# Token-major norm, an integer float64-to-float32 conversion, 1 KB loads and a fixed engine order in a linear-attention and gated feed-forward kernel

## The chip, the cores and the metric

The kernel runs on one core of one Trainium2 chip. The metric is the device time of one execution in microseconds (us), as the median of several executions. A profile shows one such execution; its span is some 2 us shorter than the device time.

TensorE (PE in the profile) multiplies matrices, PEld is its weight load, VectorE (DVE) and ScalarE (ACT) do elementwise work, GpSimd (POOL) likewise, and SyncE (SP) issues the transfers (DMA).

## The reference

```python
# q, k, v: 8 batches x 8 heads x 576 tokens x 64, float32; w1, w2: 512 x 1024, w3: 1024 x 1024,
# w_out: 1024 x 512. The four weights arrive as float64.
kv  = einsum('bhsd,bhse->bhde', k, v)
o   = einsum('bhsd,bhde->bhse', q, kv)
o   = o / sqrt(mean(o*o, axis=-1) + 1e-6) * g_norm          # norm of each token and head
x   = o.transpose(0, 2, 1, 3).reshape(8 * 576, 512)
out = ((x @ w1) * (x @ w2)) @ w3 @ w_out                     # 4608 x 512
```

Both kernels compute `w3 @ w_out` once ("the fold") and then need, for each group of 512 tokens, the gates (`x w1` times `x w2`, eight blocks of 128 features) and one projection. There are nine groups: the first 512 tokens of each batch, and one that gathers the 64 tokens left over in each.

## The kernel before

The conversion takes float64 as raw 32-bit words. Six of its operations are VectorE's, one is ScalarE's, two are GpSimd's.

```python
def convert(dst, src):                       # 128 partitions x 512 values, 40 times
    raw = fold.tile([P, c, n], I64, name="raw", bufs=3)
    nc.sync.dma_start(out=raw, in_=src)
    ...
    nc.scalar.activation(rest, lo, AF.Copy, scale=2.0 ** -52)
    nc.vector.tensor_scalar(out=bits, in0=hi, scalar1=0x7FFFFFFF, ..., op0=ALU.bitwise_and)
    nc.vector.tensor_scalar(out=power, in0=power, scalar1=LEAST, scalar2=MOST, ...)   # clamp
    ...                                      # three more on VectorE
    nc.vector.tensor_scalar(out=bits, in0=dst_bits, scalar1=0xFF800000, ...)
    nc.gpsimd.tensor_tensor(out=rest, in0=rest, in1=power, op=ALU.mult)
    nc.gpsimd.tensor_tensor(out=dst, in0=dst, in1=rest, op=ALU.add)

w1_sb = const.tile([P, NP, DF], FP32, name="w1_sb")       # NP = 4 strips of DF = 1024 columns
def convert_gates(f):
    cols = slice(f * P, (f + 1) * P)                      # block f: 128 columns of each strip
    for dst, src in ((w1_sb, w1), (w2_sb, w2)):
        convert(dst[:, :, cols], src[:, cols].rearrange("(c p) f -> p c f", p=P))
```

The norm works on features in partitions. A matmul with a matrix of 1/64 gives every feature the mean of its head, and the root and reciprocal run on 128x512:

```python
nc.tensor.matmul(ms_ps[:, 0:n], lhsT=mean_bd, rhs=sq[:, 0:n], start=True, stop=True)
nc.scalar.activation(inv[:, 0:n], ms_ps[:, 0:n], AF.Sqrt, bias=eps_col)
nc.vector.reciprocal(inv[:, 0:n], inv[:, 0:n])
nc.vector.scalar_tensor_tensor(out=dst, in0=src, scalar=g_col, in1=by, op0=ALU.mult, op1=ALU.mult)
```

The order in the program is not the order on the engines here: a scheduler in the compiler moves instructions within each engine's queue as the dependencies allow.

```python
for T in range(NG):                    # the gates of group T, with pieces of attention T+1 between
    for f in range(KF):
        gate(T, f)
        if T == 0: convert_out(f)
        if f < len(pieces): pieces[f]()
    ...
    if T == 0:
        turn_w3(0)                     # convert and transpose one block of w3
        for i in range(KF):
            if i + 1 < KF: turn_w3(i + 1)
            fold_block(i)
    project(T)
```

Of the kernel before, what the change touches and what calls it, by code (L numbers as in the profile page):

```python
# [14 lines left out]
ALU = mybir.AluOpType  # L15


@with_exitstack
def kernel(
# [12 lines left out]
    """Linear attention with per-head RMS norm, then ((x w1) * (x w2)) (w3 w_out), all in fp32.  # L32

    Weights of float64 come as their raw words and are rounded to fp32 on the chip.
    Activations stay transposed (features on partitions) from the attention to the gates.
    A group of tokens is the first 512 of one batch; the last group gathers the 64 tokens
    left over in each batch.
    """
# [7 lines left out]
    NP = H // 2          # pairs of heads: 128 features each  # L46
    KF = DF // P
    J = 4
    G = J * P            # tokens of a group
    L = S - G            # tokens left over in a batch  # L50
    KR = 96              # rows of k and v on partitions
    KJ = S // KR
    NG = B + 1
    assert D == 64 and DM == NP * P and DM == 512 and B * L == G and S % KR == 0
# [12 lines left out]
    def load_batch(b):  # L67
        k_sb = inp.tile([KR, H, KJ, D], FP32, name="k_sb")
        v_sb = inp.tile([KR, H, KJ, D], FP32, name="v_sb")
        for dst, src in ((k_sb, k), (v_sb, v)):  # L70
            nc.sync.dma_start(
                out=dst.rearrange("p h j d -> p h (j d)"),
                in_=src[b].rearrange("h (p j) d -> p h (j d)", j=KJ),
            )
        q_sb = inp.tile([P, J, H, D], FP32, name="q_sb")
        for j in range(J):
            nc.sync.dma_start(  # L77
                out=q_sb[:, j], in_=q[b, :, j * P:(j + 1) * P, :].rearrange("h p d -> p h d")
            )
        ql_sb = inp.tile([L, H, D], FP32, name="ql_sb")  # L80
        nc.sync.dma_start(out=ql_sb, in_=q[b, :, G:S, :].rearrange("h p d -> p h d"))
        return q_sb, ql_sb, k_sb, v_sb

    loaded = {0: load_batch(0)}

    g_col = const.tile([P, 1], FP32, name="g_col")
    g_src = g_norm.rearrange("(d o) -> d o", o=1)
    for e in range(2):
        nc.sync.dma_start(out=g_col[e * D:(e + 1) * D, :], in_=g_src)
# [7 lines left out]
    # |hi| is clamped to the exponents that fp32 has, so far smaller values become 0. Its low  # L97
    # 27 bits and the top bit of its exponent then make the fp32 with a 20-bit mantissa, and
    # lo, scaled by the power of two in it, is added with one rounding.
# [4 lines left out]
    def convert(dst, src):  # L104
        if src.dtype == FP32:
            nc.sync.dma_start(out=dst, in_=src)
            return
        c, n = dst.shape[1:]
        raw = fold.tile([P, c, n], I64, name="raw", bufs=3)
        nc.sync.dma_start(out=raw, in_=src)  # L110
        words = raw.bitcast(U32).rearrange("p c (n w) -> p c n w", w=2)
        lo, hi = words[:, :, :, 0], words[:, :, :, 1]
        power = fold.tile([P, c, n], FP32, name="power")
        rest = fold.tile([P, c, n], FP32, name="rest")
        bits, dst_bits = power.bitcast(U32), dst.bitcast(U32)
        nc.scalar.activation(rest, lo, AF.Copy, scale=2.0 ** -52)  # L116
        nc.vector.tensor_scalar(  # L117
            out=bits, in0=hi, scalar1=0x7FFFFFFF, scalar2=None, op0=ALU.bitwise_and
        )
        nc.vector.tensor_scalar(  # L120
            out=power, in0=power, scalar1=LEAST, scalar2=MOST, op0=ALU.max, op1=ALU.min
        )
        nc.vector.tensor_scalar(  # L123
            out=bits, in0=bits, scalar1=3, scalar2=0x40000000,
            op0=ALU.logical_shift_left, op1=ALU.bitwise_xor,
        )
        nc.vector.tensor_scalar(  # L127
            out=dst_bits, in0=hi, scalar1=0x80000000, scalar2=None, op0=ALU.bitwise_and
        )
        nc.vector.scalar_tensor_tensor(  # L130
            out=dst_bits, in0=bits, scalar=0x7FFFFFFF, in1=dst_bits,
            op0=ALU.bitwise_and, op1=ALU.bitwise_or,
        )
        nc.vector.tensor_scalar(  # L134
            out=bits, in0=dst_bits, scalar1=0xFF800000, scalar2=None, op0=ALU.bitwise_and
        )
        nc.gpsimd.tensor_tensor(out=rest, in0=rest, in1=power, op=ALU.mult)  # L137
        nc.gpsimd.tensor_tensor(out=dst, in0=dst, in1=rest, op=ALU.add)  # L138

    def convert_gates(f):  # L140
        cols = slice(f * P, (f + 1) * P)
        for dst, src in ((w1_sb, w1), (w2_sb, w2)):
            convert(dst[:, :, cols], src[:, cols].rearrange("(c p) f -> p c f", p=P))

    def convert_out(f):
        convert(wo_sb[:, f:f + 1, :], w_out[f * P:(f + 1) * P, :].rearrange("p (c f) -> p c f", c=1))

# [5 lines left out]
    mean_bd = const.tile([P, P], FP32, name="mean_bd")  # L153
    nc.vector.memset(mean_bd, 0.0)
    for e in range(2):
        rows = slice(e * D, (e + 1) * D)
        nc.vector.memset(mean_bd[rows, rows], 1.0 / D)
    kv_bd = [const.tile([P, NP, P], FP32, name=f"kv_bd{i}") for i in range(2)]
    for t in kv_bd:
        nc.vector.memset(t, 0.0)  # L160

# [4 lines left out]
    def attention(b):  # L166
        q_sb, ql_sb, k_sb, v_sb = loaded.pop(b)
        bd = kv_bd[b % 2]
        qT = work.tile([P, NP, S], FP32, name="qT", bufs=1)
        x = xT[b] = work.tile([P, NP, G], FP32, name="xT")  # L170

        def kv():
            kv_ps = bank(ps_at, "at")[:, 0:NP * D].rearrange("p (r e) -> p r e", r=NP)
            for r in range(NP):
                for j in range(KJ):
                    for e in range(2):
                        nc.tensor.matmul(  # L177
                            kv_ps[e * D:(e + 1) * D, r, :],
                            lhsT=k_sb[:, 2 * r + e, j, :],
                            rhs=v_sb[:, 2 * r + e, j, :],  # L180
                            start=(j == 0),
                            stop=(j == KJ - 1),
                        )
            for e in range(2):
                rows = slice(e * D, (e + 1) * D)
                nc.vector.tensor_copy(out=bd[rows, :, rows], in_=kv_ps[rows])

        def q_t(r):
            qt_ps = bank(ps_at, "at")
            for j in range(J):  # L190
                nc.tensor.transpose(  # L191
                    qt_ps[:, j * P:(j + 1) * P], q_sb[:, j, 2 * r:2 * r + 2, :], ident
                )
            nc.scalar.copy(qT[:, r, 0:G], qt_ps)

        def q_t_left():
            qt_ps = bank(ps_at, "at")[:, 0:NP * L].rearrange("p (r t) -> p r t", r=NP)
            for r in range(NP):
                nc.tensor.transpose(
                    qt_ps[:, r, :], ql_sb[:, 2 * r:2 * r + 2, :], ident[0:L, 0:L]  # L200
                )
            nc.scalar.copy(qT[:, :, G:S], qt_ps)
# [3 lines left out]
        def product(r):  # L206
            """o = q kv of one pair of heads (of all, for the tokens left over), and its squares"""
            o_ps = bank(ps_at, "at")
            n = G
            if r < NP:  # L210
                nc.tensor.matmul(o_ps, lhsT=bd[:, r, :], rhs=qT[:, r, 0:G], start=True, stop=True)  # L211
            else:
                n = NP * L
                for i in range(NP):
                    nc.tensor.matmul(
                        o_ps[:, i * L:(i + 1) * L],
                        lhsT=bd[:, i, :],
                        rhs=qT[:, i, G:S],
                        start=True,
                        stop=True,  # L220
                    )
            sq = work.tile([P, G], FP32, name="sq")
            nc.scalar.activation(sq[:, 0:n], o_ps[:, 0:n], AF.Square)  # L223
            st[r] = o_ps, sq, n

        def norm(r):
            """x = o * g / sqrt(mean(o^2) + eps); the means reach every feature of their head"""
            o_ps, sq, n = st.pop(r)
            ms_ps = bank(ps_at, "at")
            nc.tensor.matmul(ms_ps[:, 0:n], lhsT=mean_bd, rhs=sq[:, 0:n], start=True, stop=True)  # L230
            inv = sq
            nc.scalar.activation(inv[:, 0:n], ms_ps[:, 0:n], AF.Sqrt, bias=eps_col)  # L232
# [166 lines left out]
```

## Time and profile before

| | before |
|---|---|
| device time, median of three | 1032.11 us (1030.88 to 1033.82) |
| span of the profiled execution | 1029.5 us |
| PE busy | 937.1 us (91%) |
| VectorE / ScalarE / GpSimd busy | 377.0 / 153.0 / 108.0 us |
| first gate matmul / first fold block / end of the fold | 52.7 / 185.7 / 260.8 us |

The stages are read from two views: PE in order of time, and the chain of waits (the chain that ended last, from start to end). The busy share of the whole span hides that two stages have different limits. The groups of the page show who holds whom in the front. Each row has the line, engine, operation, output and inputs, shapes and count; then the busy us and the mean ns of one; then the idle time just ahead, with its releaser:

```profile
L137 POOL TENSOR_TENSOR rest<-rest,power 128x512 f32<-128x512 f32 x40 | 53.1, 1334 | 135.5 <-DVE power L134 130.3
L138 POOL TENSOR_TENSOR w_sb<-w_sb,rest 128x512 f32<-128x512 f32 x32 | 43.5, 1366 | 1.6
L268 PE MATMUL mm<-xT,w_sb 128*128 128x512 f32 x1024 | 457.0, 600 | 38.6 <-DVE xT L240 38.6
```

GpSimd waits 130.3 us in all for the last VectorE operation of a unit (one piece of 128x512 values), so the conversion is a chain over both engines. The gate matmuls (L268), however, are not seen to wait for weights. Their 38.6 us are spent waiting for `xT`, the last operation of the norm, which stands in the same VectorE queue as the conversion and the wide reciprocals. So it is VectorE's queue as a whole that sets when gates can run; what the conversion's share is worth is measured below (55 us).

### The profile page before, as it was taken

The page shows a single profiled execution, that of the slowest core. Times are in us where ns is not written, and L with a number is a line of the kernel's source. Part 1 is how long each engine was busy: PE and PEld are TensorE (multiplying, and loading weights), DVE is VectorE, ACT ScalarE, POOL GpSimd, SP SyncE. Part 2 cuts the span into 40 slices and gives each one's busy share as a digit, 9 for nine tenths or more (in the row PEclk, how much of TensorE's full clock was granted, in tenths as well). Part 3 has the DMA queues.
Part 4 walks back from the last instruction along what each step waited for, and adds up shares of the span by engine and source line. Part 5 has one row for each costly group of instructions (what it writes and reads, how often), then busy time and mean ns, then how long its engine had stood idle before and what let it go on. Part 6 is the DMA issues. An engine that isn't in the chain of part 4 may idle for free.

```text
span 1029.5 us, 7522 instructions
## 1 busy us (share of the span) xinstructions
PE 937.1 (91%) x3056; PEld 438.9 (43%) x3056; DVE 377.0 (37%) x448; ACT 153.0 (15%) x260; POOL 108.0 (10%) x86
## 2 busy tenths in 40 slices
PE   3138869788999999999999999999999999999997
PEld 3014425333444445444444544454444444444443
DVE  2999897884003501440053025113501440000100
ACT  2222223210001101110120122012101210000000
POOL 0555550543000000000000000000000000000000
PEclk9668969899999999999999999999999999999999
DMA  9854741830000016002500420051010000001001
GB/s 199 214 143 140 182 128 33 212 116 3 20 21 0 0 41 133 6 8 61 111 0 21 108 51 0 29 115 35 1 41 1 0 21 20 1 0 41 0 1 41
DMA packets 67075, 59.21 MB, mean 58 GB/s; under 512 B 38880, under 2 KB 59360, under 8 KB 67040
## 3 DMA queue, kind: packets, MB, share of 16 engines
q1 hardware_dynamic: 67040, 58.73, 22.7%
q8 instruction: 24, 0.39, 0.2%
q14 instruction: 11, 0.09, 0.0%
HBM read 49.28 MB, written 9.44 MB: 57 GB/s over the span
## 4 chain that ended last, share of the span: by engine, by line
PE 81%; DVE 11%; issue 3%; POOL 2%; SPq 2%; DMA 1%; ACT 0%; POOLq 0%; DVEq 0%
PE mm L268 45%; PE mm L318 24%; PE mm L306 4%; PE at L230 2%; PE at L211 2%; DVE power L117 2%; DVE power L123 1%; PE at L177 1%; DVE power L120 1%; DVE w_sb L130 1%; DVE w_sb L127 1%; POOL w_sb L138 1%; SPq L77 1%; DVE sq L233 1%; PE at L191 1%
## 5 line engine op out<-in xcount | busy, mean ns | idle before, releaser
L268 PE MATMUL mm<-xT,w_sb 128*128 128x512 f32 x1024 | 457.0, 600 | 38.6 <-DVE xT L240 38.6
L268 PEld LDWEIGHTS mm<-xT,w_sb 128*128 128x128 f32 x1024 | 195.6, 193 | 280.6 <-issue 258.7
L318 PE MATMUL mm<-w3o_sb,ab 128*128 128x512 f32 x576 | 250.0, 593 | 0.0
L279 DVE TENSOR_TENSOR ab<-a_sb,mm 128x512 f32<-128x512 f32 x72 | 49.5, 687 | 414.1 <-PE mm L268 382.7
L318 PEld LDWEIGHTS mm<-w3o_sb,ab 128*128 128x128 f32 x576 | 109.0, 190 | 132.3 <-issue 130.3
L233 DVE RECIPROCAL sq<-sq 128x512 f32<-128x512 f32 (+1 forms) x40 | 120.2, 3020 | 21.4 <-ACT sq L232 21.4
L277 ACT COPY a_sb<-mm 128x512 f32<-128x512 f32 x72 | 42.1, 585 | 279.7 <-PE mm L268 279.7
L137 POOL TENSOR_TENSOR rest<-rest,power 128x512 f32<-128x512 f32 x40 | 53.1, 1334 | 135.5 <-DVE power L134 130.3
L328 DVE COPY o_sb<-mm 128x512 f32<-128x512 f32 x18 | 12.5, 692 | 145.0 <-PE mm L318 145.0
L306 PE MATMUL mm<-wo_sb,w3T 128*128 128x512 f32 x128 | 58.0, 609 | 0.0
L268 PE MATMUL mm<-x_left,w_sb 128*128 128x512 f32 x128 | 55.1, 592 | 0.0
L230 PE MATMUL at<-sq,mean_bd 128*128 128x512 f32 (+1 forms) x80 | 41.6, 604 | 11.1 <-ACT sq L223 11.1
L326 ACT COPY o_sb<-mm 128x512 f32<-128x512 f32 x18 | 10.5, 586 | 252.7 <-PE mm L318 252.7
L116 ACT ACTIVATE rest<-raw 128x512 f32<-128x512 uint32 x40 | 27.2, 680 | 129.1 <-POOL w_sb L138 100.0
L138 POOL TENSOR_TENSOR w_sb<-w_sb,rest 128x512 f32<-128x512 f32 x32 | 43.5, 1366 | 1.6
L232 ACT ACTIVATE sq<-at,eps_col 128x512 f32<-128x512 f32 (+1 forms) x40 | 25.7, 644 | 105.8 <-PE at L230 105.6
L177 PE MATMUL at<-v_sb,k_sb 96*64 96x64 f32 x768 | 26.3, 234 | 15.1 <-DMA v_sb<-in_v_dram 14.1
L211 PE MATMUL at<-qT,kv_bd 128*128 128x512 f32 x64 | 35.6, 639 | 2.5 <-DVE xT L240 1.8
L268 PEld LDWEIGHTS mm<-x_left,w_sb 128*128 128x128 f32 x128 | 24.3, 190 | 30.6 <-issue 30.6
L306 PEld LDWEIGHTS mm<-wo_sb,w3T 128*128 128x128 f32 x128 | 24.6, 197 | 28.4 <-issue 28.4
L117 DVE TENSOR_SCALAR power<-raw 128x512 uint32<-128x512 uint32 x40 | 29.4, 735 | 12.4 <-POOL rest L137 10.1
L177 PEld LDWEIGHTS at<-v_sb,k_sb 96*64 96x64 f32 x768 | 25.2, 148 | 20.0 <-issue 17.8
(40 smaller groups left out, 347.4 us busy)
## 6 DMA issues: line engine op xcount, KB each, us to landing
raw<-in_moe_w_dram SPq DMA_DIRECT2D x32, 512.0 KB, 4.1
k_sb<-in_k_dram SPq DMA_DIRECT2D x8, 1152.0 KB, 7.9
v_sb<-in_v_dram SPq DMA_DIRECT2D x8, 1152.0 KB, 12.4
q_sb<-in_q_dram SPq DMA_DIRECT2D x32, 256.0 KB, 4.6
out_dram<-o_sb SPq DMA_DIRECT2D x16, 512.0 KB, 2.8
raw<-in_moe_w_out_dram SPq DMA_DIRECT2D x8, 512.0 KB, 3.4
ql_sb<-in_q_dram SPq DMA_DIRECT2D x8, 128.0 KB, 4.0
out_dram<-o_sb SPq DMA_DIRECT2D x4, 256.0 KB, 3.2
```

Of the source, the lines that this page charges most:

```text
L117: nc.vector.tensor_scalar(out=bits, in0=hi, scalar1=0x7FFFFFFF, scalar2=None, op0=ALU.bitwise_and)
L137: nc.gpsimd.tensor_tensor(out=rest, in0=rest, in1=power, op=ALU.mult)
L138: nc.gpsimd.tensor_tensor(out=dst, in0=dst, in1=rest, op=ALU.add)
L177: nc.tensor.matmul(kv_ps[e * D:(e + 1) * D, r, :], lhsT=k_sb[:, 2 * r + e, j, :], rhs=v_sb[:, 2 * r + e, j, :], start=(j == 0), stop=(j == ...
L211: nc.tensor.matmul(o_ps, lhsT=bd[:, r, :], rhs=qT[:, r, 0:G], start=True, stop=True)
L230: nc.tensor.matmul(ms_ps[:, 0:n], lhsT=mean_bd, rhs=sq[:, 0:n], start=True, stop=True)
L233: nc.vector.reciprocal(inv[:, 0:n], inv[:, 0:n])
L268: nc.tensor.matmul(g_ps, lhsT=w_sb[:, c, cols], rhs=xT[T][:, c, :], start=(c == 0), stop=(c == NP - 1),)
L277: nc.scalar.copy(a_sb, prods[0])
L279: nc.vector.tensor_mul(ab[T, f], a_sb, prods[1])
L306: nc.tensor.matmul(f_ps, lhsT=t[:, j, :], rhs=wo_sb[:, j, :], start=(j == 0), stop=(j == KF - 1))
L318: nc.tensor.matmul(o_ps, lhsT=ab[T, f][:, m * P:(m + 1) * P], rhs=w3o_sb[:, f, :], start=(f == 0), stop=(f == KF - 1),)
```

## The change

The intent is to shorten the front. The conversion loses GpSimd and a third of its VectorE operations: it adds the words as integers. The norm moves to token-major layout, where root and reciprocal work on 8 values per token and not on 512, at the price of transposes of x back. k, v and q come in rows of 1 KB (before, k and v in rows of 1.5 KB and q in rows of 256 B). Finally TensorE, VectorE and ScalarE keep the order of the program: the scheduler may no longer move anything on them.

```diff
-        nc.scalar.activation(rest, lo, AF.Copy, scale=2.0 ** -52)
-        ... six operations on VectorE ...
-        nc.gpsimd.tensor_tensor(out=rest, in0=rest, in1=power, op=ALU.mult)
-        nc.gpsimd.tensor_tensor(out=dst, in0=dst, in1=rest, op=ALU.add)
+        nc.scalar.activation(low, lo, AF.Copy, scale=2.0 ** -51, bias=2.0)
+        nc.scalar.activation(dst, hi.bitcast(FP32), AF.Abs)
+        nc.vector.tensor_scalar(out=dst, in0=dst, scalar1=LEAST, scalar2=MOST, op0=ALU.max, op1=ALU.min)
+        nc.vector.tensor_scalar(out=dst_bits, in0=dst_bits, scalar1=3, ..., op0=ALU.logical_shift_left)
+        nc.vector.scalar_tensor_tensor(out=low_bits, in0=hi, scalar=0x80000000, in1=low_bits,
+            op0=ALU.bitwise_and, op1=ALU.bitwise_or)
+        nc.vector.tensor_tensor(out=dst_bits, in0=dst_bits, in1=low_bits, op=ALU.add)   # uint32
...
-            nc.tensor.matmul(ms_ps[:, 0:n], lhsT=mean_bd, rhs=sq[:, 0:n], start=True, stop=True)
-            nc.scalar.activation(inv[:, 0:n], ms_ps[:, 0:n], AF.Sqrt, bias=eps_col)
+            nc.vector.tensor_reduce(out=inv, in_=sq[...], axis=AX.X, op=ALU.add)        # 128x8
+            nc.scalar.activation(inv, inv, AF.Sqrt, scale=1.0 / D, bias=eps_col)
...
+    ctx.enter_context(tc.manual_schedule(
+        engines={mybir.EngineType.PE, mybir.EngineType.DVE, mybir.EngineType.Activation}))
...
     for T in range(NG):
         for f in range(KF):
+            if T == 0 and f + 1 < KF:
+                convert_gates(f + 1)          # the next block's weights, ahead of this gate
+                ...
             gate(T, f)
...
-            turn_w3(0)
+            turn_w3(0, load_w3(0))
             for i in range(KF):
                 if i + 1 < KF:
-                    turn_w3(i + 1)
+                    turn_w3(i + 1, load_w3(i + 1))
                 fold_block(i)
```

k and v now lie on 128 partitions with four tokens each, plus a tile of 64 partitions with the 64 tokens left over, where before 576 tokens were six on each of 96 partitions. The left-over tokens are handled once in two batches, raw weights have four buffers in place of three, and the output is stored in pieces of 256 KB in place of 512 KB.

## The prediction

> **What bounds the kernel now.** I read the slices first, then the windows, then the chain of waits, then each engine in order of time.
>
> The page's slices (each is 25.7 us; digits are tenths busy, PEclk tenths of the full TensorE clock):
>
> ```profile
> PE   3138869788999999999999999999999999999997
> DVE  2999897884003501440053025113501440000100
> POOL 0555550543000000000000000000000000000000
> PEclk9668969899999999999999999999999999999999
> ```
>
> Two stages stand side by side. Up to about slice 10 VectorE (DVE) is full and TensorE (PE) is not; from there PE is full and nothing else is. A window inside the second stage (span, then busy us of each engine, clock, DMA) agrees:
>
> ```profile
> 475.00:571.00 96.00, 96.00 (x335) 45.48 (x334) 25.98 (x22) 14.32 (x25) 0.00 (x0) 1.00 0.22 48
> ```
>
> The chain of waits has the end of w3 w_out (the fold) at 260.8 us and the last matmul at 1024.0, so: front 260.8, back 763.3, tail 5.5 us. In the back a matmul record of 128x512 costs 429 ns (64 in 27.47 us). A group of tokens has 128 gate records and 64 projection records, 82.4 us; its period in the chain is 96.08, so 13.7 us of attention matmuls lie on the path. PE in order of time shows what these are (start, us):
>
> ```profile
> 481.70 3.02 PE L177 MATMUL at<-v_sb,k_sb 96*64 96x64 f32 x96
> 484.65 7.13 PE L268 MATMUL mm<-xT,w_sb 128*128 128x512 f32 x16
> 491.62 1.04 PE L191 MATMUL at<-ident,q_sb 128*128 128x128 f32 x8
> 492.49 7.03 PE L268 MATMUL mm<-xT,w_sb 128*128 128x512 f32 x16
> ```
>
> From start to start, kv is 2.95 us for 96 records (31 ns each) and a transpose is 0.87/8 = 109 ns. In the same view the product takes 0.86 us per pair of heads, the mean-square matmul another 0.86 (3.87 with the left-over tokens), and the 8 left-over products of 64 columns 0.84, so 105 ns a record.
>
> In the front the limit is conversion of float64 weights, 40 units of 128x512, on DVE and GpSimd (POOL). In order of time:
>
> ```profile
> 27.13 1.49 DVE L123 TENSOR_SCALAR power<-power 128x512 uint32<-128x512 uint32 x1
> 28.54 0.41 DVE L117 TENSOR_SCALAR power<-raw 128x512 uint32<-128x512 uint32 x1
> 28.87 0.68 DVE L130 SCALAR_TENSOR_TENSOR w_sb<-power,w_sb 128x512 uint32<-128x512 uint32 x1
> ```
>
> A tensor_scalar costs 0.41 us, or 1.49 when a POOL multiply or add (1.3 us) runs beside it. DVE also spends 120.2 us on 40 wide reciprocals:
>
> ```profile
> L233 DVE RECIPROCAL sq<-sq 128x512 f32<-128x512 f32 (+1 forms) x40 | 120.2, 3020 | 21.4 <-ACT sq L232 21.4
> ```
>
> **What the Trainium skill says.** "SBUF — State Buffer", section "SBUF: two separate sides", calls the port pair of VectorE and GpSimd an exclusive lock; 1.49 against 0.41 us agrees. "VectorE: DVE Perf Modes", "The perf-mode tier table", gives fp32 tensor_scalar two elements a cycle and tensor_tensor one; 0.41 against 0.69 us agrees. "TensorE: Matmul & The Clock Gate", "HAM oscillation — how this bites in real kernels", has PE fall to half clock after gaps of some 3 us; here PE stands still from 142 us, and after the 3.53 us gap that ends at 145.46 records take twice as long (clock 0.50 from 146 to 148). "DMA: Bandwidth & Descriptors", "Specifications", asks for at least 512 B: this trace does not show that loss, since the stretch with the 256 B q loads (17 to 21 us) moved 271 GB/s.
>
> **The change, part by part.**
>
> *Token-major norm.* Per batch it removes the mean-square matmuls (3.87 us of PE), the wide reciprocals (about 15 us of DVE) and the wide square roots. It adds four tensor_reduce and multiplies, some 1.4 us of DVE each, and 16 transposes back, 16 x 109 ns = 1.74 us of PE. The product becomes 32 records of 128 columns; at the 105 to 109 ns seen for narrow records that is 3.5 us, as before (3.44). kv has 80 records for 96: 2.46 for 2.95. q transposes stay at 1.74. Left-over tokens come once in two batches: 8 transposes (0.9) and 32 records of 64x64, which I put at 55 ns, 1.8 us. Sum: even batch 2.46+1.74+3.5+1.74 = 9.4, odd 12.1, mean 10.8 us against 13.7.
>
> *Back.* In the fixed order each attention piece has a 6.9 us gate between it and the next, and its longest chain (square, reduce, root, reciprocal, multiply) is about 3.5 us, so PE should not wait. Nine projections 247.2, eight groups of gates 439.5, six batches 64.8: 751.5 us against 763.3. It saves only 12 us, because the old scheduler had already put 5 us of batch 2 into the front; a fixed order keeps all of it in the back.
>
> *Conversion.* No POOL; ScalarE two passes (about 0.58 us apart); DVE four operations: two tensor_scalar, one scalar_tensor_tensor, one tensor_tensor. With dependent spacing from the trace: 0.46+0.34+0.73+0.60 = 2.13 us a unit, against 167 us/40 = 4.2 before (five rows of L117 to L134 summed). That is 82 us of DVE saved, if DVE is kept fed.
>
> *Loads.* The bytes before v lands are the same 2.36 MB, which took until 14.1 us. 1 KB rows: no gain on the path.
>
> *Fixed order, front.* I followed the three engines through the program. kv 14 to 18.4 (54 ns a record, cold, as before), q at 19; four product-norm turns at about 2.6 us each with one gate conversion in line, then the last turns: first gate near 39 us (before 52.7, then starved). Gates 0 to 3: 6.9 us each, since DVE needs 0.9+4.3 in between, plus 1.7 cold: done at 68. Gates 4 to 7 also carry w_out units and attention(1) on the same DVE queue. With four raw buffers a w_out load of gates 4 and 5 cannot start until the second unit of the pair in front is read; landing is 3.4 to 4.1 us, and DVE stands behind it. I get gate 7 ending at 119. Then one w_out unit, the left-over norms, three w_out units, four w3 units and their copies: first fold at 145 us.
>
> *Fixed order, fold.* This is where the gain goes. The program puts turn_w3(i+1) ahead of fold(i) on PE, and the copy of fold(i) ahead of the conversion for i+2 on DVE. Each then waits for the other: copy 0.9, unit 2.1, hop and transposes 0.9, copy 0.9, unit 2.2, transposes 0.8, fold 6.87 = 14.5 us a block, against 10.45 before:
>
> ```profile
> 212.50 2.86 POOL L138 TENSOR_TENSOR w_sb<-w_sb,rest 128x512 f32<-128x512 f32 x2
> 215.91 7.03 PE L306 MATMUL mm<-wo_sb,w3T 128*128 128x512 f32 x16
> 222.95 2.86 POOL L138 TENSOR_TENSOR w_sb<-w_sb,rest 128x512 f32<-128x512 f32 x2
> 226.36 7.03 PE L306 MATMUL mm<-wo_sb,w3T 128*128 128x512 f32 x16
> ```
>
> The PE gaps (3.2 us twice, short transposes between) are near those that halved the clock; a cold fold costs about 2.1 us more and its transposes 0.9: 17.4 us. I take 16.5, i.e. mostly cold. Six such blocks 99, last two folds 9.0+6.9, copy 0.9: the front ends at 145+115.8 = 260.8, where it ends today. DVE work was halved and put in series.
>
> Sum: 260.8 + 751.5 + 5.3 (tail) = **1017.6 us**, called 1018, 1.4% below 1032.
>
> **Rivals.** (a) Fold stays warm: 14.5 a block, front about 247, total 1004. For it: the gaps hold transposes, and today's 10.45 us blocks stay at clock 1.00. Against: 3.53 us sufficed at 145. (b) The front is as good as its sums: PE alone needs 55+55 us for gates and fold and some 25 for attention and transposes; gates unhindered and the fold at 14.5 would make 977. Against it: every queue is in order, and the chains above cross engines several times per gate. (c) A new wait grows: loads of batches 1 and 2 (3.5 MB each, 16 us at 215 GB/s) queue ahead of the w_out loads and hold DVE 4 to 10 us more, with all folds cold: 1035 to 1042. (d) In the back, narrow records bound by weight loading at 190 instead of 109 ns would add 2.6 us per batch, 16 in all; the 105 ns of today's narrow records speak against it.
>
> **Range and chances.** Cold and warm fold differ by 6 x 3 = 18 us, the start of the fold is known to some 12 us, the back to 6. Combined that gives 990 to 1042. The line for "faster by 2%" is 1011.8, reached only if the fold is warm or the gates run freer: 0.30. Within 2%: 0.64. Slower by over 2% (above 1053) needs a wait that I did not find: 0.06.
>
> **What would show it.** POOL idle; DVE tensor_scalars all near 0.41 us; reciprocals tiny. First gate near 39, first fold near 145, end of fold near 261, with a fold every 14.5 to 17.4 us and PE waiting for VectorE between. Records of 855 ns in the folds if cold. Back periods near 92 and 94.5 us with PE full. The prediction is wrong if folds come every 10 us or less (then the engines overlap where I say they cannot), if the gates of group 0 end before 110, or if the back period stays at 96.

## The result, and the profile after

| | before | after |
|---|---|---|
| device time, median of four | 1031.83 us (1030.88 to 1033.82) | 1056.60 us (1054.93 to 1057.48) |
| profiled span | 1029.5 us | 1053.1 us |
| first gate | 52.7 | 37.4 |
| gates of group 0 done | 168.9 | 140.7 |
| first fold block | 185.7 | 172.4 |
| end of the fold | 260.8 | 289.6 |
| from there to the last matmul | 763.3 | 759.0 |

The changed kernel is slower: the ratio is 1.0237, with a 95% interval of 1.0220 to 1.0254. A ratio is the mean time of one kernel's fast runs over that of the other's of the same rounds, so it is not quite the ratio of the medians quoted.

The table says where. The changed kernel is 15 us ahead at the first gate, 28 us ahead when the gates of group 0 are done, and still 13 us ahead at the first fold block. The fold itself then takes 117.2 us where before it took 75.1, and 42 us are lost. The last gate records of group 0, in the kernel before and in the changed one, are:

```profile
161.86 7.03 PE L268 MATMUL mm<-xT,w_sb 128*128 128x512 f32 x16
133.62 7.03 PE L292 MATMUL mm<-xT,w_sb 128*128 128x512 f32 x16
```

So the gates of group 0 became faster, but by less than they could. The slices of the page after (26.3 us each) show the whole front:

```profile
PE   5587745667799999999999999999999999999998
DVE  2546453332201210220121022112201210110010
POOL 0000000000000000000000000000000000000000
PEclk9789876777899999999999999999999999999999
```

In the first eleven slices no engine is full. VectorE, full in the front before, now stands at 2 to 6 tenths, and PE does not fill the space. So this front is bound by waits, not by any engine's work. The groups and PE's order of time name the first of these waits:

```profile
L292 PE MATMUL mm<-xT,w_sb 128*128 128x512 f32 x1024 | 462.9, 606 | 21.7 <-DVE w_sb L128 20.9
L316 PE MATMUL mm<-ident,w_sb 128*128 128x128 f32 x64 | 16.3, 403 | 55.9 <-DVE w_sb L128 55.9
```

```profile
37.35 2.08 PE L292 MATMUL mm<-xT,w_sb 128*128 128x512 f32 x2 [0.78 <-ACT xT L263]
40.69 9.71 PE L292 MATMUL mm<-xT,w_sb 128*128 128x512 f32 x16 [1.27 <-DVE w_sb L128]
52.53 8.83 PE L292 MATMUL mm<-xT,w_sb 128*128 128x512 f32 x16 [2.12 <-DVE w_sb L128]
```

VectorE in the same stretch:

```profile
39.95 0.69 DVE L128 CUSTOM_DVE_ANT_0 w_sb<-w_sb,low 128x1024 uint16<-128x1024 uint16 x1
51.78 0.69 DVE L128 CUSTOM_DVE_ANT_0 w_sb<-w_sb,low 128x1024 uint16<-128x1024 uint16 x1
```

This is odd. The weights of gate 0 were converted before 37 us, and its first matmul (two records) ran. Its third record then stands until 40.69, when the integer add of a w1 unit ends. By the program that unit belongs to block 1, whose weights gate 0 does not read. The same happens at 52.53: the first two records of gate 1 run, and the third waits for the first unit of block 2. (A matmul leaves two records here, so the first two read strip 0 of the block and the third reads strip 1.) Two waits are therefore to be explained: this one, and the fold. In PE's order of time, one block of the fold and the start of the next are:

```profile
188.44 9.15 PE L333 MATMUL mm<-wo_sb,w3T 128*128 128x512 f32 x16
200.59 0.63 PE L316 MATMUL mm<-ident,w_sb 128*128 128x128 f32 x4 [3.00 <-DVE w_sb L128]
204.13 1.11 PE L316 MATMUL mm<-ident,w_sb 128*128 128x128 f32 x4 [2.90 <-DVE w_sb L128]
205.03 9.38 PE L333 MATMUL mm<-wo_sb,w3T 128*128 128x512 f32 x16
```

PE waits twice per block, 3.00 and 2.90 us, for a converted unit of w3, and then runs its 16 records in 9 us and not 6.9; the granted clock from 188 to 192 us is 0.50. In the chain of waits a block comes every 16.9 us on average (six from 172.41 to 273.68).

### The profile page after: what moved, and what is told of

The parts are those of the page before. It is cut to its first block, busy times and chain, and to the rows that moved or that the text cites. A ratio compares the mean times of both kernels' runs of the same rounds, so it can differ in the third digit from the quotient of the medians.

```text
span 1053.1 us, 7803 instructions
## 1 busy us (share of the span) xinstructions
PE 945.6 (90%) x3232; PEld 465.2 (44%) x3232; DVE 229.3 (22%) x421; ACT 178.0 (17%) x332; POOL 0.7 (0%) x6
## 4 chain that ended last, share of the span: by engine, by line
PE 88%; DVE 9%; ACT 1%; DMA 1%; issue 1%; SPq 0%; DVEq 0%; ACTq 0%
PE mm L292 48%; PE mm L344 23%; PE mm L333 7%; PE at L163 3%; PE at L223 2%; DVE low L124 2%; DVE w_sb L128 2%; PE mm L316 2%; PE at L258 1%; PE at L180 1%; DVE w_sb L121 1%; DMA v_sb<-in_v_dram 1%; DVE w_sb L118 1%; DVE w3T L321 1%; DVE inv L202 0%
## 5 line engine op out<-in xcount | busy, mean ns | idle before, releaser
L292 PE MATMUL mm<-xT,w_sb 128*128 128x512 f32 x1024 | 462.9, 606 | 21.7 <-DVE w_sb L128 20.9
L333 PE MATMUL mm<-wo_sb,w3T 128*128 128x512 f32 x128 | 71.4, 723 | 0.0
L316 PE MATMUL mm<-ident,w_sb 128*128 128x128 f32 x64 | 16.3, 403 | 55.9 <-DVE w_sb L128 55.9
L223 PEld LDWEIGHTS at<-kv_bd,qT 128*128 128x128 f32 x256 | 34.1, 197 | 16.2 <-issue 12.4
L200 ACT ACTIVATE sq<-at 128x512 f32<-128x512 f32 (+1 forms) x40 | 22.1, 552 | 100.2 <-PE at L223 99.1
L223 PE MATMUL at<-kv_bd,qT 128*128 128x128 f32 x256 | 35.2, 282 | 3.0 <-ACT xT L263 2.7
L163 PE MATMUL at<-v_sb,k_sb 128*64 128x64 f32 x512 | 23.7, 240 | 11.5 <-DMA v_sb<-in_v_dram 11.5
L258 PE MATMUL at<-ident,xn 128*128 128x128 f32 x144 | 22.6, 285 | 10.6 <-DVE xn L210 9.9
L202 DVE TENSOR_REDUCE inv<-sq 128x8 f32<-128x512 f32 (+1 forms) x40 | 25.2, 631 | 26.7 <-ACT sq L200 26.7
L263 ACT ACTIVATE xT<-at,g_col 128x512 f32<-128x512 f32 x32 | 21.7, 677 | 42.8 <-PE at L258 42.8
L116 ACT ACTIVATE low<-raw 128x512 f32<-128x512 uint32 x40 | 26.5, 662 | 7.3 <-DVE wo_sb L128 6.4
```

The costliest lines, as they stand in the source:

```text
L116: nc.scalar.activation(low, lo, AF.Copy, scale=2.0 ** -51, bias=2.0)
L163: nc.tensor.matmul(kv_ps[e * D:(e + 1) * D, r, :], lhsT=k_sb[:, h, cols] if j < J else kl_sb[:, h, :], rhs=v_sb[:, h, cols] if j < J else ...
L200: nc.scalar.activation(sq[:, cols], o_ps[:, cols], AF.Square)
L202: nc.vector.tensor_reduce(out=inv, in_=sq[:, cols].rearrange("p (h d) -> p h d", d=D), axis=AX.X, op=ALU.add,)
L223: nc.tensor.matmul(o_ps[:, h * P:(h + 1) * P], lhsT=qT[i, half][:, h, :], rhs=bd[:, half * HB + h, :], start=True, stop=True,)
L258: nc.tensor.transpose(t_ps[:, r, :], xn[:, 2 * r:2 * r + 2, :], ident)
```

## The experiments

Each kernel was run in three rounds beside the kernel before on the same chip, and each gave a correct result. The kernel before took 1030.9 to 1031.8 us in all of these sets, so runs of different sets can be compared to about 1 us. The theory at this point had two parts. **Gates:** the integer add, which the profile names `CUSTOM_DVE_ANT_0`, makes readers of other blocks wait, because its output is booked from its first to its last element. The 128-column blocks of the wide tile interleave in that extent. Strip 0 of a block lies ahead of everything that the next block writes, which would be why the first two records of a gate run. **Fold:** the program's order puts VectorE and PE in series, as predicted. The rivals were that the gates are limited by the conversion's own length or late raw weights, and that the fold is slow because of transfers.

### One tile per block of w1 and w2

```diff
-    w1_sb = const.tile([P, NP, DF], FP32, name="w1_sb")
+    w1_sb = [const.tile([P, NP, P], FP32, name=f"w1_sb{f}") for f in range(KF)]
...                                            # w2_sb the same
-                    lhsT=w_sb[:, c, cols],
+                    lhsT=w_sb[f][:, c, :],
-            convert(w_sb[:, :, f * P:(f + 1) * P], raw)
+            convert(w_sb[f], raw)
```

> The changed kernel with one edit: each block of 128 gate columns of w1 and w2 gets a tile of its own instead of a slice of one wide tile. Theory A: in the changed kernel the third record of each gate of group 0 waits for the conversion of the NEXT block, because a column block of the wide tile is four strips, and the strips of the next block interleave with those that the gate reads, so that the program waits as if they overlapped. With tiles apart these waits (20.9 us, plus the half-clock restarts they cause) go: the stretch of the eight gates falls from 103 to about 80 us and the total from 1056 to about 1030. Rival B: the gates are late because VectorE's queue in fixed order (gate multiply, then conversion) sets the pace anyway: less than 5 us change.

Measured: 1030.33 us (1029.44 to 1030.92), 26 us less than the changed kernel; ratio to before 0.9996 (0.9981 to 1.0011). PE in order of time:

```profile
37.64 30.05 PE L291 MATMUL mm<-xT,w_sb 128*128 128x512 f32 x64 [0.78 <-ACT xT L263]
```

All 64 records of gates 0 to 3 now run in one row, and the last gate of the group ends at 116.7 us and not at 140.7. The instructions, their order and their durations are those of the changed kernel. The conversion's length and the raw weights were therefore not the limit.

### One tile, but each block contiguous in it

```diff
-    w1_sb = const.tile([P, NP, DF], FP32, name="w1_sb")
+    w1_sb = const.tile([P, KF, NP, P], FP32, name="w1_sb")
...
-                    lhsT=w_sb[:, c, cols],
+                    lhsT=w_sb[:, f, c, :],
```

> The changed kernel, w1 and w2 still one tile each, but laid out block by block, so that the 128 columns of one block are contiguous and the extents of two blocks no longer interleave. If the false wait comes from the extents (first to last element) of interleaved strips, it goes as with separate tiles: total about 1030, gates of group 0 in about 79 us. If whatever is in one tile waits for all of it, the total stays at 1056.

Measured: 1029.66 us (1029.46 to 1030.45), ratio 0.9988 (0.9973 to 1.0002). The number of tiles does not matter; whether the extents of two blocks overlap does.

### Another operation in place of the integer add

The wide tile stays, and the add becomes an ordinary bitwise operation of the same length. Every converted weight then has the wrong sign. All four weight matrices enter the output as a product, so the four signs cancel.

```diff
-        nc.vector.tensor_tensor(out=dst_bits, in0=dst_bits, in1=low_bits, op=ALU.add)
+        nc.vector.tensor_tensor(out=dst_bits, in0=dst_bits, in1=low_bits, op=ALU.bitwise_xor)
```

> The changed kernel, wide tiles kept, with the last step of the conversion as an ordinary bitwise xor in place of the integer add. All four weights come out with their sign turned and within a unit or so in the 20th bit, and the four signs cancel in the result. The kernel before wrote the same interleaved strips with ordinary instructions, and there matmuls of strip c=1 ran (76.5 us) well before the last block was converted (103 us). If only the custom instruction of the integer add is tracked by its extent, the waits go and the total is about 1030. If interleaved strips cause it with any instruction, it stays at about 1056.

Measured: 1029.64 us (1028.21 to 1030.32), ratio 0.9984 (0.9969 to 0.9999). The same tile, the same strips and the same order lose the wait when the operation is not the integer add:

```profile
36.63 29.64 PE L292 MATMUL mm<-xT,w_sb 128*128 128x512 f32 x64 [0.78 <-ACT xT L263]
```

These three runs fit one reading: a false dependency of the integer add, over its extent. How the compiler books it is not in a trace; that contiguous blocks or another operation each remove it is.

### The fold in another order

```diff
             for i in range(KF):
-                if i + 1 < KF:
-                    turn_w3(i + 1, load_w3(i + 1))   # convert, transpose and copy block i+1
-                fold_block(i)                        # matmuls and copy of block i
+                if i + 2 < KF:
+                    convert_w3(i + 2)                # VectorE has block i+2 ready ahead of time
+                fold_block(i)                        # matmuls i; transposes and copies of i+2; copy i
```

> The changed kernel with one edit: in the fold the conversion of w3 block i+2 is put before the matmuls of fold i, and its transposes after them, with the copy of fold i last. Theory: the fold is slow (16.9 us a block) only because TensorE and VectorE each stand behind the other in the fixed order; now a block should take 8 to 9 us (6.87 of matmuls, 0.9 of transposes), at full clock, and the total fall by 45 to 60 us to about 1000. Rival: the conversions themselves (VectorE 4.3 us a block, ScalarE, or the loads of w3) set the pace: blocks stay at 12 us or more and the total above 1030.

Measured: 997.29 us (996.01 to 998.55), 59 us less than the changed kernel; ratio 0.9676 (0.9662 to 0.9691). The chain of waits:

```profile
168.79 8.60 PE mm L340 x16
177.40 0.87 PE mm L323 x8
178.27 6.87 PE mm L340 x16
185.14 0.87 PE mm L323 x8
186.01 6.87 PE mm L340 x16
```

A block costs 7.74 us, which is its matmuls and transposes and nothing else, and from 175 us the granted clock is 1.00. Per block that is 9.1 us less than 16.9. Six such blocks make 55 us, and the first block starts 3.6 us earlier (168.8 for 172.4). The loads are the same, so transfers were not the cause.

### Both repairs, in the fixed order

The edit is the sum of the first and the fourth.

> The changed kernel with both mends, separate gate tiles and the reordered fold, order still fixed. If the two losses are independent they add: 1056 - 26 - 59 = about 971. If one hides the other, 980 or more. Still well above the free order (938), since the queues of VectorE and ScalarE stay in program order while attention and w_out are mixed into the gates.

Measured: 970.28 us (969.06 to 972.09), ratio 0.9406 (0.9391 to 0.9422). The two gains are independent: 1056.6 − 26.3 − 59.3 = 971.0.

### The changed kernel without the fixed order

```diff
-    ctx.enter_context(
-        tc.manual_schedule(
-            engines={mybir.EngineType.PE, mybir.EngineType.DVE, mybir.EngineType.Activation}
-        )
-    )
```

> The changed kernel with the fixed order taken away: the scheduler orders TensorE, VectorE and ScalarE again, as in the kernel before. If the fixed order is the cause, the fold overlaps again (8 to 11 us a block) and the total falls to 990 to 1020, while the waits of the gates of group 0 for the next conversion stay if they come from the shared tile (theory A). If the order is not the cause, it stays near 1055.

Measured: 937.62 us (936.08 to 940.19), ratio 0.9104 (0.9086 to 0.9123): 119 us less than the changed kernel, with neither cause repaired by hand. This is far below what was expected (990 to 1020), and the waits of the gates, which were expected to stay, are gone. First PE's slices, then rows of PE in order of time and of the chain of waits:

```profile
PE   4799899999999999999999999999999999999998
```

```profile
34.58 30.04 PE L292 MATMUL mm<-xT,w_sb 128*128 128x512 f32 x64 [0.93 <-ACT xT L263]
...
112.53 6.87 PE mm L333 x16
120.27 6.87 PE mm L333 x16
```

The scheduler makes both repairs itself. It moves conversions ahead of the gates that falsely need them (both adds of block 1 end by 36.5 us, where the fixed order ends them at 40.6 and 42.8; the adds of blocks 2 to 4, too, end before the second matmul of the gate in front reads that tile), and it keeps fold blocks 7.74 us apart. It also fills group 0 better: PE is nearly full from the third slice on, and the fold ends at 172.7 us, where the repaired fixed order ends it at 206.8.

### Both repairs and no fixed order

> Both mends without the fixed order. If the scheduler had already got around both losses by running conversion ahead, this is within 1% of the free order alone (938): 930 to 940. If the false wait still costs it something, 925 or less.

Measured: 935.45 us (935.03 to 936.24), ratio 0.9073 (0.9060 to 0.9087). The repairs add next to nothing to a free order: their intervals of the ratio (0.9060 to 0.9087 and 0.9086 to 0.9123) just touch. The 34.8 us from 970.28 to 935.45 is what remains of the fixed order once its two worst points are mended.

### The kernel before with the integer conversion alone

The edit is the conversion's part of the diff above and nothing else; the order is the scheduler's.

> The kernel before with the integer weight conversion alone. If the front of the kernel before was set by conversion on VectorE under GpSimd's lock (4.2 us of VectorE a unit against 2.1 now), the front falls from 261 to some 200 us and the total to 960 to 1000. Rival: the front is set by the wide reciprocals and the order of the norm, and the total stays within 20 us of 1032.

Measured: 976.00 us (975.19 to 976.56), ratio 0.9469 (0.9455 to 0.9483). So 55 us come from the conversion alone. The end of the fold moves from 260.8 to 204.3 us, and the back does not change. Its gates look as if the false wait were here too, which the next run tests. The last gate conversion, and the long row of gate records (this view ends at 100 us and cuts the row there):

```profile
76.08 0.69 DVE L127 CUSTOM_DVE_ANT_0 w_sb<-w_sb,low 128x1024 uint16<-128x1024 uint16 x1
```

```profile
78.18 22.05 PE L257 MATMUL mm<-xT,w_sb 128*128 128x512 f32 x51
```

Up to there PE had run only ten gate records, in pieces of two to four.

### The same with one tile per block

> The kernel before with the integer conversion and one tile per 128-column block of w1 and w2. In the run with the integer conversion alone (976.0 us) the long row of gate records began at 78.2 us, just after the last gate conversion at 76.8. Theory (false wait through the custom integer add): the long row of gates starts well before the last gate conversion and the time falls, to 955 to 970 us. Rival (VectorE is the limit there and the wait is met anyway): 976 within 4 us. In either case what is left against 933.6 us is what norm, loads and left-over tokens of the redesign are worth in a free order.

Measured: 962.67 us (961.42 to 965.75), ratio 0.9341 (0.9317 to 0.9365), 13 us less. Gates now run between the conversions, though the last gate conversion comes no sooner (76.8 us): 48 gate records start before 78.2 us, against ten. One row of eight in PE's order of time:

```profile
41.44 3.60 PE L256 MATMUL mm<-xT,w_sb 128*128 128x512 f32 x8
```

Here, unlike in the redesign, the scheduler had not got around the false wait. The 962.67 us also tell what the rest of the redesign is worth in a free order: 962.67 − 935.45 = 27 us. That is norm, loads, left-over tokens, buffers, stores and the order of the pieces together; no run takes them apart.

### A control: one tile per block in the kernel before

> The kernel before with one tile per 128-column block of w1 and w2, nothing else. Theory (only the custom integer add makes the false wait, and this kernel writes the strips with ordinary operations): no change, 1031 within 4 us, and the first gates still wait for VectorE and GpSimd. Rival (any write to a strip of the wide tile makes later readers of another block wait): the gates start earlier, 1015 or less.

Measured: 1032.79 us (1030.91 to 1033.59), ratio 1.0011 (0.9994 to 1.0028). Nothing changes. A kernel that writes the strips with ordinary operations does not have the false wait, so the layout became a cost only with the integer add.

### The order of k-v matmuls

In the back, kv took 3.51 us per batch where 2.46 were predicted. PE in order of time, in the changed kernel:

```profile
323.90 0.69 PE L163 MATMUL at<-v_sb,k_sb 128*64 128x64 f32 x16
324.52 0.33 PE L163 MATMUL at<-vl_sb,kl_sb 64*64 64x64 f32 x4
324.78 0.69 PE L163 MATMUL at<-v_sb,k_sb 128*64 128x64 f32 x16
```

From start to start, 16 records of 128 rows take 0.62 us (39 ns each) and 4 of 64 rows take 0.26 (65 ns). The theory is that each change between row counts costs a fixed time. The edit lets two pairs of heads share it; the kernel is the changed one with a free order and one tile per block.

```diff
-                for j in range(J + 1):
+                order = list(range(J + 1)) if r % 2 == 0 else [J] + list(range(J))
+                for j in order:
```

> Free order and separate gate tiles (the fold as the changed kernel has it), and in the k-v products of every second pair of heads the chunk of 64 left-over rows goes first instead of last, so that TensorE passes 4 times instead of 7 between matmuls of 128 rows and of 64 rows in a batch. In the changed kernel 16 records of 128 rows take 0.62 us and 4 of 64 rows 0.26 us; at 31 ns a record they would take 0.49 and 0.12, so each passage seems to cost 0.13 us. If so, k-v of a batch falls from 3.51 to about 3.1 us and the total to about 932. If the price lies in the records themselves (rows), k-v stays at 3.5 us and the total at 935.

Measured: 933.55 us (930.97 to 934.68), ratio 0.9055 (0.9040 to 0.9070). The total does not separate it from 935.45 us, but the rows do:

```profile
295.96 0.45 PE L164 MATMUL at<-vl_sb,kl_sb 64*64 64x64 f32 x8
296.34 1.15 PE L164 MATMUL at<-v_sb,k_sb 128*64 128x64 f32 x32
297.42 0.45 PE L164 MATMUL at<-vl_sb,kl_sb 64*64 64x64 f32 x8
```

32 records of 128 rows take 1.08 us from start to start, 16 take 0.62: the second 16 cost 29 ns each, and some 0.15 us is left over for each block, whether of 16 or 32 records. The same holds for 8 and 4 records of 64 rows (0.38 and 0.26). With 80 × 29 ns = 2.32 us, eight blocks give 3.5 and five give 3.1; the chain has 3.51 and 3.07. This version has the lowest median of all, some 9.5% below the kernel before. No run separates the number of rows from the change of tile (`k_sb` to `kl_sb`) that comes with it.

## Why the prediction was wrong

The prediction said 1018 us, from 990 to 1042, most likely within 2% of before. It is 1056.6 us, slower by 2.4%. The prediction gave that outcome a chance of 0.06 and tied it to "a wait that I did not find", which is what happened. Of its signs of being wrong none came true: they asked for a faster front or an unchanged back, and a late gate 7 was not among them. The terms of its sum, against the profiled span of 1053.1 us:

| term | predicted | measured | difference |
|---|---|---|---|
| start to the first gate | 39 | 37.4 | −1.6 |
| gates of group 0 ("gate 7 ending at 119") | 80 | 103.3 | **+23.3** |
| gate 7 to the first fold | 26 | 31.7 | +5.7 |
| fold | 115.8 | 117.2 | +1.4 |
| back | 751.5 | 759.0 | +7.5 |
| tail | 5.3 | 4.5 | −0.8 |
| sum | 1017.6 | 1053.1 | +35.5 |

**The step that failed** is "Gates 0 to 3: 6.9 us each, since DVE needs 0.9+4.3 in between, plus 1.7 cold: done at 68". Its arithmetic was right: with one tile per block the four gates run from 37.6 to 67.7, where the changed kernel ends them at 81.1, and gate 7 ends at 116.7. It assumed that a gate waits for its own weights alone. It did not ask which writes the compiler would take for writes to those weights, and rival (c), "A new wait grows", looked for it in transfers. In a free order such a wait may be met by moving other work in between. In the fixed order it stands in line, seven times, for 20.9 us of PE idle, and costs 26 us in all.

**The fold** was right in cause and size: VectorE and PE in series, mostly cold, at 16.9 us a block against 16.5. (The terms of its warm block add to 14.7 us, not 14.5, which would put six blocks 1 us higher.) The claim on the clock (PE falls to half clock after gaps; the page says some 3.4 us, the prediction "some 3"), which leaned on the Trainium skill's "TensorE: Matmul & The Clock Gate", section "HAM oscillation — how this bites in real kernels", holds too: 16 records took 9 us after gaps of 3 us, and 6.87 us at clock 1.00 once the order left no gaps. Rivals (a) and (b) did not come about.

**The conversion** was right: a unit takes 2.13 us on VectorE, GpSimd is idle, and the tensor_scalars take 0.41 to 0.43 us. Alone it is worth 55 us. The fixed order took it all back.

**The back** was right in kind (PE full, periods of 93.18 and 95.71 us for 91.8 and 94.5 predicted) and mis-sized in one term. kv was put at 31 ns a record for 80 records, 2.46 us. It took 3.51, because the records alternate between 128 and 64 rows; six batches make 6.3 of the 7.5 us. Rival (d) did not come about: 8 narrow records of the product take 0.89 us in the chain, 111 ns each.

**Between gate 7 and the fold** 5.7 us more than predicted passed. With one tile per block the stretch is as long (116.7 to 148.4 us), so the false wait is not the cause. On the chain ScalarE's two passes stand in line twice (147.6 to 149.5 and 163.3 to 165.0 us) and four groups of transposes take 1.1 us each; the cause stays open.

**The loads** were a small miss the other way: "1 KB rows: no gain on the path" put the first k-v matmul at 14.1 us, and it started at 11.5. The prediction read no loss from the 256 B loads of q out of a window (17 to 21 us) that also holds weights in rows of 1 KB. Taken apart, the same trace shows one: from 14 to 18 us all packets are of some 250 B and 214 GB/s move with the DMA engines full, and from 19.2 to 22 us, with packets of some 1 KB, 346 GB/s. In the kernel before, packets of q are mixed with k and v on the way to the first matmul. No run separates this from the 128 partitions in place of 96. From the first k-v matmul to the first gate 24.9 us were predicted and 25.9 passed, so two small misses partly cancel in the first row of the table.

The prediction followed the fixed order and found that it would eat the gain; the experiments put a size on that. Taking the fixed order away is worth 119 us, of which the two waits in the program are 86 us and its poorer filling of group 0 the rest (with both waits repaired the fold still ends 34 us later).

## What to carry to other kernels

Fixing the order of several engines by hand is worth trying only against the free order on the same kernel: here the scheduler beat the program by 119 us, and by 35 us after the two worst places were repaired. When a loop prepares block i+1 and consumes block i, write it so that each engine's queue reaches the preparation of i+2 ahead of the work that waits for i, otherwise two engines take turns and the matmul clock falls as well. When an operation is replaced by one of the same length, look at the first wait of its neighbours for a releaser that the data flow does not explain; giving each block a contiguous piece of memory is a cheap test.

## What the Trainium skill lacked or had wrong

- No page found says what a uint32 tensor_tensor add becomes on VectorE. Here it ran as a custom instruction on 128x1024 uint16, 0.69 us for 128x512 words, and it makes readers of other, interleaved blocks wait: 20.9 us of PE waits in group 0, and 26 us of the time. A bitwise operation of the same shape does not.
- "VectorE: DVE Perf Modes", section "Specifications", calls integer operands "exact only below 2^24". The add here has words far above that (bit patterns of float32 with their exponent) and took 692 ns, as recorded on uint16 halves. The outputs pass, but no run here tests whether its sums are exact, so the section is not refuted; it is silent on this instruction.
- "TensorE: Matmul & The Clock Gate", section "HAM oscillation — how this bites in real kernels", has the clock fall after idle gaps of more than some 3.4 us. Here two gaps of 2.90 and 3.00 us per block, with 0.6 to 1.1 us of transposes between and beside them, were enough: 16 records took 9 us in place of 6.87.
- "TensorEngine Tiling (Array Packing)", section "Key Properties", says that changing the tiling mode drains TensorE, without a price. The runs fit this and give one, if the drain is the cause: about 0.15 us for each change between matmuls of 128 rows and of 64 rows in k-v, against 29 ns for one such matmul.
